# One core, DeltaNet then a normalised MLP: another order of the kernel's 3032 steps, with one filler less

## The chip, the cores and the metric

One core of one Trainium2 chip. The metric is the device time of the core in microseconds. The kernel before was timed three times: the median is 517.51 us, the lowest time 514.65 and the highest 519.48.

## The reference

All data are fp32. An attention block without softmax (the delta rule) is followed by a layer norm and an MLP with a residual.

```
q, k, v: (4 batches, 8 heads, 768 tokens, 48)   beta: (4, 8, 768)
k_n = k / (norm(k) + 1e-6); state = 0
for t in range(768):
    y[t]  = q[t] @ state
    state = state + beta[t] * outer(k_n[t], v[t] - k_n[t] @ state)
x   = y with heads joined               # (4, 768, 384)
xn  = (x - mean) / sqrt(var + 1e-6) * g_ln
out = x + relu(xn @ w_ch1) @ w_ch2      # 384 -> 1536 -> 384
```

## The kernel before, in words

The 768 tokens are cut into 12 chunks of 64. A chunk holds 64 tokens of all 4 batches, so 256 rows; its two halves (g = 0 and g = 1) are the 128 rows of two batches each. Inside a chunk the sequential rule becomes a triangular system: a Gram matrix of the keys, the inverse of a unit lower triangular matrix, products of that inverse with the values (u), and products of u with the queries' block (y). Only a state of 48 x 48 per head goes from chunk to chunk.

Chunk 0 has no state before it and nothing to overlap with, so it is done first and by itself. Its inverse is built in five doubling rounds on TensorE (products E1 to E5 and Z1 to Z5, lines 769 and 785), with masked copies and transposes on VectorE (lines 774 and 734) and copies out of PSUM on ScalarE (line 728), for two groups of eight heads in turn. Chunk 1 uses a Gram matrix that goes out to DRAM and comes back by rows (tile `gb`), and a row-by-row inverse on VectorE (lines 896 to 913). The later chunks use the same row-by-row inverse, in pairs, in five such stages that VectorE works through while TensorE does the MLP of earlier chunks. From chunk 3 on the MLP products are made from sums and differences of blocks, formed on VectorE and GpSimd (lines 1289, 1329, 1509, 1547), with fewer products on TensorE (lines 1306 and 1522).

The MLP weights are loaded and written anew as sums of two parts, by ScalarE (lines 591 and 599), VectorE (596) and GpSimd (609). The first MLP products of a chunk are 12 of 6 matmuls; in chunk 0 they are made for each half by itself, 24 in all (line 1405), each followed by a ReLU on ScalarE (line 1413).

**The order.** The kernel is first written down as a list of steps, numbered 0 to 3031. A step is one group of instructions on one engine (32 matmuls, one copy, one DMA) with the steps that must be done before it. Nothing of this list is executed in the order of its numbers: the string `ORDER`, some 100 lines of step numbers and ranges, says in which order the steps are emitted, and `Line.emit` goes through it word for word. It asserts that every step comes once and after all it depends on. `in_this_order` (line 23) then holds every engine to this order, and all DMAs of SP and ScalarE to one order among each other. So the engines run side by side, each through its own queue, and what the string decides is which step stands ahead of which in each queue.

Two words of the string are no steps. "f" and "F" are **fillers** (function `idle`, line 1595): a matmul of the identity matrix into a bank that the next TensorE step overwrites anyway, over 128 columns for "f" and 512 for "F". They compute nothing.

```
        n = 512 if size == "F" else 128
        nc.tensor.matmul(banks_of[key][:, 0:n], ident, ident[:, 0:1].to_broadcast([128, n]))
```

One more thing follows from the order: GpSimd's computing steps wait for the last VectorE step ahead of them in the string that is marked `port`, the normalising step of line 1150 among them (the dependency "shared port" in `Line.emit`).

The steps that the change and the prediction speak of:

| steps | engine, line | what they do |
|---|---|---|
| 201, 197 | TensorE 785 | last products of chunk 0's inverse (Z5), one for each group of heads |
| 181-183, 187-189; 198-200, 202-204 | ScalarE 728 | copies of Z4 and of Z5 out of PSUM |
| 191, 193 | VectorE 774 | last masked copies of the inverse |
| 236, 240, 242 | ScalarE 591, 599 | weight conversions over 768 columns |
| 259 | ScalarE 882 | square root on chunk 1's rows, waits for the loads of `gb` |
| 305 | SP 409 | one load of later keys (tile `kr`) |
| 329, 331 | TensorE 1068 | u of chunk 0, first and second half |
| 330, 332 | VectorE 1073 | scaling of u |
| 333, 334 | TensorE 1094 | y of chunk 0 (its output), first and second half |
| 335, 336 | ScalarE 1132 | y out of PSUM into x |
| 337-346 | VectorE, ScalarE | layer norm of both halves; 343 and 346 (line 1150) write the normalised halves |
| 309, 310, 321, 322 | TensorE 627 | key transposes of chunks 2 and 3 |
| 311, 312, 323, 324 | ScalarE 632 | the copies of these |
| 313, 325 | TensorE 818 | Gram products of chunks 2 (G2) and 3 (G3); 314, 315 and 326, 327 copy them out (ScalarE 839) |
| 353, 354 | TensorE 1104, ScalarE 1116 | state after chunk 0, and its copy |
| 426, 427 | TensorE 627 | query transposes of chunk 1 (428, 429 copy them, ScalarE 632) |
| 347, 351 | TensorE 1182 | transposes of the normalised first and second half |
| 348-350, 352 | ScalarE 1198, VectorE 1188 | the scaled transposes, copied out of PSUM |
| 567, 569, 571, ... 589 | TensorE 1405 | chunk 0's first MLP products, first half; 591 to 613 those of the second |
| 213, 217, 225, 229 | GpSimd 609 | last step of the conversion of four parts of the first weight |
| 366, 372, 378, ... | GpSimd 609 | the same for the second weight |

Of the kernel before, what the change touches and what calls it, by code (L numbers as in the profile page):

```python
# [174 lines left out]
682 781 1082 647 651 648-649 683-686 689 688 690 1084 1086 1069 837-838 833-834 843 793 1175 923 928 920 925 927 919 691 545-546  # L175
692-696 687 697 650 698-700 795 839 550 549 548 547 551 555 554 840 552-553 1091 1081 1083 845-846 848 847 1079 829-830 854 796
835 797 855-856 800 836 844 801 798 929 652 701 930 1176 931 643-644 1179 1181 628 1182 1172 1171 921 1183 918 629 1178 1180
1184-1185 556 802 702-704 1075 841 857-859 799 932 557 922 842 805 705 806 706-709 803-804 849-850 852 851 1085 463 864-868 860
871 933 807 810 559 561 558 869 560 934 811 808 710 809 812 562 872 861-862 1542 853 863 870 813 817 881 873-875 882 876 883-886
565-566 814 563 818 820 711-712 936 1087 877 713-716 564 816 815 819 935 937-938 879 1544 1554 887 1556 880 1553 888 1546 1543 878  # L180
1558 1560 1541 464 1555 1559 1557 1547 889-893 896 894 897 972 898-901 939 941 1186 717-722 895 723-725 902 940 726 1076 974
942-943 1077 975 907 1190 1088-1089 973 908-910 980-981 911-912 978 727-741 946 986 742 944-945 947 743-751 913 979 951 984-985
952 976 987 977 990-991 948-949 982 1005 992 983 988-989 1006-1010 994 1368-1370 1372 1367 1373 1078 1090 1371 1363 752 1095 1093
755-756 753 1545 1177 999-1000 996-997 1002 903 964-965 998 1012 970 1003 1013 904 967 995 1011 1187 953 955 754 915 1374 1094 757
950 954 758 1092 1650 905 956 1375 1188 1362 1653 906 1364 759 993 1022-1026 1030 1001 1004 1014 1096-1100 1102 760 762 1032
1015-1018 1033 761 763 766 1189 1034-1036 1019 1027 1037 1020 767 765 764 1103 1191 768 1192-1193 971 969 966 1219 1548 1021
1040-1045 769 1194 1652 914 960 1104 1028 1038 1196 1647 957-958 1655 959 1657 1360-1361 1029 1031 1039 968 1105 1047-1050 771-773
770 1106 1046 1058-1060 1107-1111 1195 774 1376 1198 963 962 1197 961 1199 1201-1202 1200 1549 1220 1234 1061-1062 1051 1227 1223
1238 1221 1366 776 1206 777 1203 778 1052 775 1228 1063 1207 1112 1377-1378 1208 1053 1064 1231-1232 1235 1659 1365 1656 1658 1654
1239 1236 1229-1230 1237 1055 1246 1224 1242 1247 1222 1225 1379 1210 1561 1204-1205 1380 1113 1381 1240 2030 1261 1233 1209 1660  # L190
1241 1114-1117 1243 1248 1244 1249 1245 1262 1275 1280 1270 1054 1226 1250 1118 1255 1258 1256 1259 1257 1382 1263-1264 1266-1267
1265 1260 1271-1272 1251 1119 1268 1281-1282 1273 1120-1121 1269 1283 1122-1124 1066 1211 1845 1212-1214 1284 1274 1308-1309 1057
1841 1215 1218 1065 1056 1844 1847 1849 1851 1646 2042 1252 1285 1253 1286 1310 1276 1383 1311 1277 1287-1288 1312 1298-1299 1254
1313 1278 1314 1292 1289-1291 1295-1296 1305 1300-1302 1333 1325-1326 1303-1304 1279 1334-1335 1315-1316 1336 1293 1306 1327 1294
1297 1337-1338 1307 1328 1317-1318 1329-1330 1322 2044 1323 1319-1320 1648 1850 1645 1839 1125-1129 1384 1339 1130-1131 1331 1324
1351-1356 1217 1216 2032 1332 1340-1343 1550 1344-1345 1415 2029 1419 1408-1410 2034 2033 1423 1551 1562 1411 1563 2031 1132-1135
1357 1385 1661 1424 2035 2046 2043 1136-1137 1321 1412-1413 1427 1138-1142 1346 1143-1165 1552 1564 1837-1838 1166 1567 1569 1566
1169 1168 1167 1170 1414 1416 1420 1417 1425 1418 1426 1432 1439 1421 1440 1433 1428-1430 1451 1442 1461 1443 1348 2036 1456 1422
1436-1437 1431 1438 1387 1444-1445 1447-1448 1101 1441 1434 1446 1435 1449 1452-1454 1457 1462-1463 1651 1565 1464 1450 1386 1455
1458 1479-1480 1466-1467 1481 1489 1482-1483 1490 1484 1491 1465 1662 1473 1347 2045 1470-1471 1674 1568 1388 1390-1391 1485 2047  # L200
1389 1468-1469 1474 1472 1476 1475 1459 1663-1664 2037 1395 1392 1667 1665 1460 1570 1666 1492-1494 1496-1499 1350 1349 1358 1848
1393 1396 1394 1397 1495 1571 1399 1398 1676 1668-1669 1671 1670 1672-1673 2041 1514 1500 1515 1477 1516 1486 1501 1487 1675 1677
1506-1509 1478 1488 1510-1511 1517 1503 1843 2048 1504 1518-1519 1649 1359 1846 1400 1402 1852 1401 1404 1403 1855 1572-1574 1577
1576 1512 1578 1502 1678 1681 1520 1683 1579-1580 1407 1405 1679 1406 1505 1513 1682 1704 1680 1686-1687 1691 1581-1585 1532-1533
1521-1523 1534 1524-1525 1705 1535-1536 1856 1853 1526 1586-1588 1684 1589 1685 1590-1591 1857-1860 1537 1706 1708 1692 1854 1709
1719 1715 1711 1723 1866 1861 1592 1527-1528 1707 1710 1538 1688 1863-1864 1862 1712-1713 1716-1717 1714 1720-1722 2049 1593 1747
1724 1529 1725-1726 1728 1840 2141 2135 2143 2145 1540 2328 1738 1757 1752 1739 1689-1690 1594 1694 1718 1727 1868 1732 1729 1733
1735-1736 1734 1740-1741 1743-1744 2142 2147 1530 2140 1842 2144 1531 2146 2137 1539 2133 1595 1693 1695-1696 1698-1699 1697 1700
# [1543 lines left out]
```

## Time and profile before

| | us |
|---|---|
| median of three runs (lowest, highest) | 517.51 (514.65, 519.48) |
| the execution that was profiled | 517.98 |
| its span in the trace | 516.2 |
| mean granted TensorE clock | 0.982 |
| TensorE busy | 484.4 (94% of the span) |
| VectorE busy | 360.4 (70%) |
| GpSimd busy | 280.4 (54%) |
| ScalarE busy | 206.5 (40%) |

The profiled execution took 0.47 us more than the median; some 1.8 us of it lie outside the span. The profile gives busy times and waits of each engine, and the trace behind it every instruction. A wait is named after what ended it; "issue" means that an engine stood still for nothing that the profile shows.

### The profile page before, as it was taken

The numbers are of one execution on the slowest core, as the hardware profiler recorded it, in microseconds if no ns is written. First come the engines' busy times: TensorE is split into PE (matmuls) and PEld (weight loads), VectorE is DVE, ScalarE is ACT, GpSimd is POOL, SyncE is SP. The second block draws the span as 40 slices with busy tenths as digits, with TensorE's granted clock in tenths as the row PEclk, the third lists the DMA queues.
The fourth block names the chain that finished last, engine by engine and source line by source line (L and its number), as shares of the span: only waits on it lengthen the run. The fifth ranks groups of instructions, "written<-read, shape, count | busy, mean of one in ns | idle before, by whom it ended". The sixth has DMA issues, their size and how long they took to land.

```text
span 516.2 us, 22793 instructions
## 1 busy us (share of the span) xinstructions
PE 484.4 (94%) x9970; PEld 448.6 (87%) x9970; DVE 360.4 (70%) x814; ACT 206.5 (40%) x462; POOL 280.4 (54%) x447
## 2 busy tenths in 40 slices
PE   4576898999999999999999999999999999999997
PEld 4454798678898898999989999999999999999996
DVE  6685548798899579979778998877688527253241
ACT  4685654632542234232443441444423344434130
POOL 7033455263477598777592354555444723654544
PEclk9898699999999999999999999999999999999999
DMA  9978477488626845354743554733440702212011
GB/s 136 258 161 211 143 126 175 107 190 153 117 46 117 181 109 91 75 109 114 148 106 64 119 109 97 150 80 64 103 79 24 160 19 57 62 36 60 2 39 30
DMA packets 181635, 54.56 MB, mean 106 GB/s; under 512 B 164888, under 2 KB 177312, under 8 KB 181536
## 3 DMA queue, kind: packets, MB, share of 16 engines
q1 hardware_dynamic: 168512, 40.10, 38.1%
q10 hardware_dynamic: 10816, 9.83, 6.7%
q0 software_dynamic: 2208, 3.17, 3.8%
q8 instruction: 78, 1.28, 1.0%
q14 instruction: 21, 0.17, 0.1%
HBM read 36.30 MB, written 16.78 MB: 103 GB/s over the span
## 4 chain that ended last, share of the span: by engine, by line
PE 80%; DVE 6%; DMA 5%; issue 3%; SPq 2%; ACT 2%; POOL 0%; ACTq 0%; DVEq 0%; POOLq 0%
PE f L1522 27%; PE f L1306 21%; PE f L1425 6%; PE two L818 4%; PE f L1405 3%; PE f L1447 3%; SPq L409 2%; PE by L1032 2%; PE by L1094 2%; PE two L1032 2%; PE two L1104 2%; PE two L1087 2%; DMA gb<-gd 2%; DMA gd<-gsb 1%; PE f L627 1%
## 5 line engine op out<-in xcount | busy, mean ns | idle before, releaser
L1509 POOL TENSOR_TENSOR h_all<-h_all 128x256 f32<-128x256 f32 x99 | 72.0, 740 | 21.5 <-DVE tmp L906 10.2
L1522 PE MATMUL f<-w_sb,h_all 128*128 128x192 f32 x396 | 80.0, 329 | 0.0
L1522 PE MATMUL f<-words,h_all 128*128 128x192 f32 x396 | 78.5, 330 | 0.0
L1329 DVE TENSOR_TENSOR h_all<-f,h_all 128x512 f32<-128x512 f32 x72 | 48.7, 685 | 27.5 <-PE f L1306 20.4
L1522 PEld LDWEIGHTS f<-w_sb,h_all 128*128 128x128 f32 x396 | 65.3, 190 | 1.4 <-ACT h_all L1434 0.2
L1522 PEld LDWEIGHTS f<-words,h_all 128*128 128x128 f32 x396 | 65.0, 190 | 0.9 <-issue 0.2
L1324 ACT COPY h_all<-f 128x512 f32<-128x512 f32 x45 | 26.1, 586 | 74.0 <-PE f L1306 57.4
L913 DVE TENSOR_TENSOR xb<-xb,tmp 128x31 f32<-128x31 f32 (+19 forms) x139 | 52.8, 380 | 3.5
L1547 POOL TENSOR_TENSOR words<-h_all 128x128 f32<-128x128 f32 x66 | 29.4, 468 | 46.8 <-ACT h_all L1333 23.2
L906 DVE TENSOR_TENSOR tmp<-xb,gb 128x31 f32<-128x31 f32 (+19 forms) x139 | 49.7, 357 | 3.9 <-POOL xb L893 0.3
L1333 ACT ACTIVATE h_all<-h_all 128x512 f32<-128x512 f32 x54 | 33.0, 628 | 25.2 <-DVE h_all L1329 24.9
L409 POOL DMA_DIRECT2D tb<-in_k_dram x64 | 41.7, 656 | 0.3 <-issue 0.2
L1306 PE MATMUL f<-x_new,w_sb 128*128 128x128 f32 x288 | 39.6, 276 | 0.0
L1306 PE MATMUL f<-xnt,w_sb 128*128 128x128 f32 x288 | 39.0, 277 | 0.6 <-DVE h_all L1329 0.6
L1306 PEld LDWEIGHTS f<-x_new,w_sb 128*128 128x128 f32 x288 | 36.7, 192 | 0.1
L1306 PEld LDWEIGHTS f<-xnt,w_sb 128*128 128x128 f32 x288 | 35.8, 192 | 0.9 <-POOL ident L1289 0.7
L1425 PE MATMUL f<-xnt,w_sb 128*128 128x256 f32 x144 | 33.8, 383 | 0.0
L1425 PEld LDWEIGHTS f<-xnt,w_sb 128*128 128x128 f32 x144 | 26.7, 190 | 3.9
L609 POOL TENSOR_TENSOR w_sb<-words 128x768 uint32<-128x768 uint32 (+1 forms) x11 | 14.7, 1352 | 22.3 <-issue 15.0
L1522 PE MATMUL f<-w_sb,words 128*128 128x192 f32 x132 | 26.2, 332 | 0.0
L1540 DVE TENSOR_TENSOR o<-f,x 128x192 f32<-128x192 f32 x33 | 11.3, 349 | 20.0 <-PE f L1522 17.8
L1132 ACT COPY x<-by 128x384 f32<-128x384 f32 x23 | 10.4, 479 | 36.4 <-PE by L1094 22.6
(237 smaller groups left out, 997.3 us busy)
## 6 DMA issues: line engine op xcount, KB each, us to landing
words<-in_moe_w_ch_dram ACTq DMA_DIRECT2D x20, 384.0 KB, 5.2
gd<-gsb SPq DMA_DIRECT2D x11, 512.0 KB, 3.2
v<-in_v_dram SPq DMA_DIRECT2D x24, 192.0 KB, 4.6
kr<-in_k_dram SPq DMA_DIRECT2D x46, 96.0 KB, 3.5
out_dram<-o SPq DMA_DIRECT2D x46, 96.0 KB, 2.6
xld<-xlt SPq DMA_DIRECT2D x9, 384.0 KB, 2.6
xnt<-xld SPq DMA_DIRECT2D x36, 96.0 KB, 3.0
tb<-in_q_dram SPq DMA_DIRECT2D x40, 64.0 KB, 3.0
```

The source lines that it names most:

```text
L409: add(eng, cost, lambda: QUEUE[eng].dma_start(out=out_, in_=in_), r, w, bulk=n * ns / 16e3, np=n, **kw)
L818: nc.tensor.matmul(pair[hp][half(e ^ (hp & n)), (g * NP + j) * C : (g * NP + j + 1) * C], kt[drows(hp), l], rt[drows(hp), i],)
L906: lambda j=j, n=n, w=w, t=t: nc.vector.tensor_tensor(out=t, in0=xv[:, 0:n, j : j + 1].to_broadcast([128, n, w]), in1=gv[:, j : j + 1, j + ...
L913: "DVE", dve(n * w), lambda t=t, rest=rest: nc.vector.tensor_tensor(out=rest, in0=rest, in1=t, op=ALU.subtract),
L1306: nc.tensor.matmul(wide(p[:, f : f + 128]), w[:, f : f + 128], r, start=start and i == 0, stop=True, skip_group_check=True)
L1324: add("ACT", act(512), lambda: nc.scalar.copy(o, p), pk, ok)
L1329: add("DVE", dve(512), lambda: nc.vector.tensor_tensor(out=o, in0=x, in1=y, op=op), [*xk_, *yk], ok)
L1333: add("ACT", act(512), lambda: nc.scalar.activation(o, o, ACTF.Relu, scale=scale), [], ok)
L1425: nc.tensor.matmul(p[:, 0:TOK], w1_sb[:, t, f * 128 : (f + 1) * 128], xnt[:, t], start=(t == 0), stop=(t == KC - 1))
L1509: add(eng, cost, lambda: e.tensor_tensor(out=out_, in0=x, in1=y, op=op), r, w, port=2 if eng == "Pool" else 1, pr=-2)
L1522: lambda f=f, t=start and f == order[0]: nc.tensor.matmul(p[:, 0:D2], lhs(f), rhs[:, f], start=t, stop=(f == order[-1]), skip_group_check=True
L1547: lambda f=f + i: e.tensor_tensor(out=s3[f], in0=one(0, 0)[0](f), in1=one(1, 0)[0](f), op=ALU.subtract),
```

## The change

Only the string `ORDER` is another. Both strings hold each of the 3032 steps once. The one before has two fillers, "f" ahead of step 94 and "F" (two matmuls over 512 columns in the trace) ahead of step 334; the one after has one, "f" ahead of step 114.

Of TensorE's 954 steps 747 stand at another place of its queue, by 2.9 places on average; of VectorE's 814 steps 716, by 4.2; of ScalarE's 489 steps with its DMAs 368, by 2.7; of GpSimd's 443 steps 376, by 4.0; of SP's 332 DMAs 294, by 6.7. The last 60 steps of TensorE's queue stand in nearly the same order as before.

Where the first chunk goes over into its MLP, TensorE's queue reads, before and after:

```
before: 201 197 310 329 331 333 F 334 309 313 321 322 353 325 426 347 427 351 567 571 569 575 430 593
after:  197 201 329 310 309 333 331 313 321 322 353 334 325 427 426 347 567 569 571 430 351 575 593 579
```

On ScalarE the copies 187 and 181 go ahead of the square root 259, and the conversions 240 and 242 behind all six copies of Z4; 336 goes behind 354; 349 goes ahead of 428. On SP load 305 goes behind the loads of `gb`. On VectorE the norm of the second half (339, 340) goes behind the normalising step of the first (343). On GpSimd 213, 217 and 225 stand behind 343 and ahead of 229. The start of the string, where the words above stand:

```diff
--- before
+++ after
 ORDER = """
-51 53-54 52 65 9 57-58 56 55 308 63 319 398 62 306 67 66 320 7 64 10 249 11-12 2 15 14 22 13 18 0 42 8 61 40 46 654 44 41 43 60 59
-656 47 72 71 1 75-77 82 3 101-102 27 83 16 24 73 84 99 68 103 74 36 104 100 93 37 f 94 38 105-106 85 17 28 86 69 87 21 70 6 88 78
-19 79 23 20 116-117 80 118 81 110-111 120 39 107 121 108 97 119 124-125 132 25 112 134 122 90 137 135 218 205 113 230 115 133
-140-141 143 123 34 109 251 258 253 92 136 207 114 126-128 152 138 142 89 208 154 30 26 129-131 157 139 146 148 147 158 91 96 156
-155 144-145 232 150-151 220 95 149 98 206 224 305 255 257 252 256 254 395 405 317 307 402 401 396 399 318 404 48 45 49 209 153
-160-161 159 168 219 162 170 169 163 176 653 657 165 210 172 166 171 222 173 167 164 5 29 177 4 174-175 223 31-32 184 186 185 178
-231 180 179 192 190 212 226 238 188 259 182 189 181 240 183 187 225 233 221 658 50 33 193 191 260-262 194-195 201 197 236 203 242
-204 200 199 198 202 211 241 237 310 329 239 263 35 196 243 250 264 331 227 330 333 332 F 334 234-235 214 312 335 361 356 355 336
-265-266 215 337 267-272 339 273 340 338 274-294 309 311 313 362 216 314 344 315 341 321-322 353 323-324 244 228 354 342 295 343
-325-327 345 393 316 296 403 397 328 406 213 217 248 229 655 659 346 426 347 427 348 350 428 349 429 351 567-568 571 569 572 575
-666 660 302 300 299 304 467 298 468-469 303 301 466 297 400 394 352 430 593 245 431 246 570 573 247 365 576 407 579 432 363 357
-359 465 668 358 360 364 580 594 583 599 584 574 367 661 410 587 577 588 368 578 591 581 592 582 366 408-409 600 411 470 585 379
-412 586 605 597 589 606 369 590 374 598 371 413 380 611 603 595 434 471-474 477 476 478-480 370 481 414 482 415 372 670 667 672
-671 665 669 392 461 1068 1070 416 433 604 596 601 418 373 419 612 602 420 417 609 607 385 421 608 610 386 381 383 377 613-614 422
-424 423 425 375 389 615-618 630-631 435-436 632 619 633 620 783 785-787 782 784 788 917 387 437 440 442 438 475 483-502 382
-503-506 376 507-515 673 439 378 384 634-635 662 441 443-444 447 445-446 663 516 388 517 450-452 448-449 518 621-622 674 789 1174
-779-780 664 1173 1080 390 462 1072 1067 1071 391 1073 677 1074 790 519 457 453 636-641 675-676 916 520-539 681 678 924 540 680 679
-926 542 541 544 543 459 456 458 455 460 454 623 791 794 821 624-625 642 822 645-646 792 825 827 626-627 826 831-832 823-824 828
...
+52 0-1 54-55 53 51 58 57 393 56 66 320 67 63 62 308 398 306 319 65 9 61 10 59 64 249 7 5 11-14 2 44 8 40 654 60 42 45 41 43 46 248
+656 71-72 68 38 75 82 76 3 101-102 36 83-84 74 77 39 37 73 100 99 6 21 85-86 69 28 16 24 22 70 78 15 17 23 79-80 27 87 81 88 116
+18 110-111 117 19 112 103-106 93 89 122 94 207 90 f 114 107-108 120 115 113 92 121 119 206 97 109 251 253 258 118 124 31 30 20 123
+125-127 32 130 132 128 134 133 136 135 137 129 220 131 218 232 230 138 33 139-141 143 142 146 152 25 34 219 147 153 26 148 158 154
+231 91 96 222 145 144 151 156 150 157 149 208 155 95 226 228 98 214 160 159 162 223 161 164 163 168 170 29 174 169 4 176 171 167
+166 165 172-173 205 210 254 252 395 255-257 402 307 305 401 318 405 317 48 233 653 49 658 175 50 221 47 177-178 181 179 184 186
+185 192 238 236 187 259 189 188 182-183 240 242 180 190 193 191 194-195 197 201 200 198-199 235 204 203 202 209 260 211 261 241
+262-263 237 35 250 265 329 234 310 196 330 309 311 264 243 362 333 312 239 331 335 224 356 361 355 266-273 332 274 337-338 275-285
+215 286-293 313-315 321 216 322 246 353 334 212 323-324 341 244 354 342 294-295 343 336 325-327 427 426 347 316 396 399 406 296
+403 328 217 213 225 227 339 348 350 349 428 340 344-345 567 407 568 429 229 659-660 666 245 346 408 247 655 657 404 300 303 301
+304 298 466 468 299 302 467 297 469 400 397 394 569 571 570 572 430 351-352 357 363 431 575 593 576 579 573 580 583 432 409 359
+584 587 574 594 358 364 360 410 577 588 599 591 367-368 578 581 411 365-366 592 582 585 600 605 597 470 412 586 589 598 413 369
+590 379 595 371 596 374 603 661 667-668 1068 434 465 471-474 477 476 478-479 370 480 414-415 372 670-672 392 665 669 391 601 416
+606 602 604 419 418 380 611 417 612 420 373 609 607 630 433 421 385 610 608 381 386 383 424 423 422 375 425 377 631-633 615-616
+634 617 635 435-436 618-620 783 785 787-788 916 481-509 376 382 378 437 440 389 441 387 442 438 673 510-514 384 1070 439 445 388
+446 515 443 450 516-517 451 518-520 444 782 789 636-637 613 662 638-639 614 663 447 674-675 786 784 780 390 790 521 452 448-449
+522-539 779 917 664 1176 676 924 680-681 540 679 678 925-926 542 541 543-544 621-623 457 624 453 625 640-641 1072 1080 1071 1082
+458 456 460 459 455 454 794 791 626 642 821-822 645 792 627 646-647 475 648-649 651 825 827 826 831 823 832 828 837 682 833 838
+843 834 683-686 689 781 677 688 845 1069 1084 848 1074 922 463 1079 1073 1067 1086 1081 1085 824 846-847 1083 545 793 546 839 547
+550 548-549 551 554-555 553 552 829 840 830 652 690 556 687 795 927 921 928 918 920 919 923 929-930 691-695 931 650 696-701
...
```

More of the change, by code (lines that the diff above doesn't have):

```diff
@@ L177 @@
[L177 to L184, printed above, removed]
@@ new lines @@
+1173 1185 1184 841 857 932 557 858-859 851 849-850 842 807 1075 1541-1542 853 464 861 864-865 559 703 808 933 810 860 871-872 809
+813 811 704-706 812 852 863 862 1544 878 560-561 558 562 934 817 881 873-874 882 866-869 883-884 875-876 885-886 819 816 566 563
+818 820 814 564-565 815 1087 1554 1546 936 707-712 887 713-714 877 870 715-716 935 937 1556 879-880 461-462 1543 1545 1547 1186
+889-894 896-901 972 1091 888 717-722 938 723-724 939-940 895 902 941 1076 973 943 942 1077 907 974-975 908-912 1190 1088 980-981
@@ new lines @@
+978 986 979 1089 984-985 987 725-728 946 729-736 947 737-751 913 976 990 977 982 944-945 948-949 991 1005-1007 983 988 992 1008
+989 994 1009 951 993 995 1368 1172 1361 1369-1370 1372 1078 1371 1367 1648 1360 1374 752 915 1090 755 754 756 753 1094 1558 1560
+1559 1557 1548 996 903 1177 997 999 904 1187 964 998 1002 970 1000 1003 1012-1013 967 1092 914 905 1093 1174 1095 906 969 952 757
+953 950 1188 954-955 758 1015 1032-1033 1010 1034 1016-1018 1001 1004 965 1220-1221 1014 1011 1022 1019 1023-1024 760-762 759 768
@@ new lines @@
+1189 763 1191 971 966 1219 1366 1020 1035 1021 1036-1037 1040-1041 1096 765 767 766 764 1038 1047 956 1649 1039 1553 1373 960 957
+1365 958-959 1192 1048 1025 1042 1026-1027 1043 769 1375 968 1193-1194 772 771 770 961 963 1549 1653-1655 1657-1659 1656 1364 1652
+1029 1097-1100 1102 962 1234 1223 1030 1028 1227 1103-1104 1195 1031 1196 1044-1045 1049-1052 1046 1224 1053 773 1197 774 777-778
+775 1198-1200 1055 1270 1238 1376-1377 1201-1203 776 1204 1058-1063 1228 1231 1206 1064 1235 1229 1236 1232 1239-1240 1237 1242
@@ new lines @@
+1644 1641 1643 1927 1919 1924-1926 1876 1824 1930-1931 1825 1949 1944 1939 1932 1928-1929 1933 1935-1936 1934 1937 1940-1941 1945
+1950-1951 1938 1878 1942 1879 1883 1922 1943 1977-1980 1967 1952 1946 1954-1955 1968-1970 1923 1971 1953 1884 1877 1885 1887
+1880-1882 1956 2151 1947 1957-1959 1961-1962 1964 1974 2139 1963 1826 2054 2337 1827 2055 2057 2149 2152 2150 1886 2156 1972 1981
+1973 2155 1948 2154 2058 2153 1888 1836 2339 1835 2334 2338 2135 1891 1889-1890 2522 1892 1960 1965 1975 1966 1976 1982 1994-1995
@@ new lines @@
+1983-1985 2002-2003 1986 1991 2157 2162 2159 2059 1987-1989 2004-2007 2164 2053 2060-2061 2343 2062 2064-2065 2008 2066 1996
+2160-2161 2158 2163 2165-2166 1893 2020 1997-1999 2021 2167 2169 1990 2067-2069 2340 2070-2071 2000 1992 2001 1993 2063 2072 2168
+1895 2170 2172-2173 2171 2192 2174 1894 2176-2177 2073 2178 2199 2203 2175 2179 2009-2012 2022-2025 2193 2013-2014 2196-2197 2074
+2015 2200 2194 2201 2075-2076 2195 2180-2181 2016-2017 2207 2235 2211-2212 2026 2183 2077 2341 2344 2204-2205 2198 2226-2227 2202
@@ new lines @@
+2342 2182 2206 2078-2079 2525 2527 2184 2529 2524 2530 2027 2187 2517 2531 2711 2330 2528 2185-2186 2188 2018-2019 2526 2028
+2208-2209 2216 2213-2214 2210 2080-2081 2215 2082-2085 2345 2347 2346 2220-2221 2223 2222 2348 2228 2224-2225 2229 2217 2231-2232
+2086-2088 2230 2233 2236-2237 2218 2238 2349 2354 2245 2331 2240 2246-2247 2234 2219 2239 2241 2273 2242 2263 2089-2091 2248
+2092-2094 2250-2251 2274 2356 2252 2352 2351 2249 2350 2253-2254 2257 2255-2256 2264-2267 2353 2260 2258 2095-2097 2275 2268
@@ new lines @@
+2600 2621 2617 2622 2618 2623 2630 2601 2631 2602 2515 2568 2571 2569-2570 2516 2572 2632 2740 2734 2736 2657 2626 2658 2647-2648
+2659 2649-2650 2634-2635 2633 2603 2651-2652 2739 2741 2636 2627 2653 2628 2637 2660-2662 2664-2668 2574-2575 2742 2638 2641
+2639-2640 2645 2504 2506-2507 2655 2644 2654 2674 2743 2573 2766 2773 2809 2642-2643 2663 2646 2656 2675-2677 2682 2767 2683-2684
+2678 2685-2687 2679 2671-2672 2669 2688 2768 2700-2701 2680 2670 2673 2689-2690 2770 2702 2691 2781 2769 2782 2703-2704 2692-2694
@@ L253 @@
+2976 2983-2984 2987-2988 2985 2951 2964 2961-2963 2967 2965-2966 2968 2977 2989 2978 2990-2992 2889 2888 2986 2997-3000 3005 2898
+2897 3006-3007 2969 2979 3001-3002 3008 2994 3003-3004 2996 3009 3012-3014 3010 3015-3017 2995 3011 2993 3018 3023-3029 3020 3019
+3021 3030 3022 3031
 """
```

115 lines of the change are left out of this document (45 added, 70 removed).

## The prediction

> **What bounds the kernel now.** I read the page first for the engine that sets the end, then a table of stretches for the place where that engine stands idle, then the timeline of that place, engine by engine.
>
> ```profile
> span 516.2 us, 22793 instructions
> PE 484.4 (94%) x9970; PEld 448.6 (87%) x9970; DVE 360.4 (70%) x814; ACT 206.5 (40%) x462; POOL 280.4 (54%) x447
> q8 instruction: 78, 1.28, 1.0%
> PE 80%; DVE 6%; DMA 5%; issue 3%; SPq 2%; ACT 2%; POOL 0%; ACTq 0%; DVEq 0%; POOLq 0%
> kr<-in_k_dram SPq DMA_DIRECT2D x46, 96.0 KB, 3.5
> ```
>
> TensorE is busy 94% of the span and makes 80% of the chain that ended last, so the end moves only if TensorE's idle time shrinks or grows: the change removes no work but one filler. The stretches (length, then busy time of PE, PEld, DVE, ACT, POOL, then granted clock, DMA share, GB/s) say where it idles.
>
> ```profile
> 0.00:42.40 42.40, 25.63 (x866) 21.24 (x866) 31.29 (x86) 28.78 (x68) 18.12 (x35) 0.96 0.91 182
> 42.40:64.20 21.80, 16.22 (x353) 13.28 (x354) 11.30 (x44) 12.02 (x27) 8.26 (x12) 0.69 0.63 180
> 50.98:61.22 10.24, 8.88 (x221) 7.82 (x216) 6.88 (x30) 6.30 (x12) 2.71 (x4) 0.50 0.50 159
> 64.20:512.40 448.20, 442.58 (x8754) 414.12 (x8752) 317.47 (x684) 165.68 (x369) 253.98 (x402) 1.00 0.45 95
> 182.00:208.00 26.00, 25.62 (x797) 23.52 (x797) 23.19 (x37) 10.37 (x28) 21.79 (x26) 1.00 0.47 94
> ```
>
> Up to 42.4 us (chunk 0's inverse) TensorE is idle for 16.8 us, from there to the first MLP product at 64.2 for 5.6 us and at a clock of 0.69, and in the 448 us after it for 448.20 - 442.58 = 5.6 us. From 64.2 on there is almost nothing to win and much to lose; what comes earlier ahead of 64.2 shows at the end almost whole. The timeline of TensorE around it:
>
> ```profile
> 40.03 1.04 PE L785 MATMUL f<-xt,pt 64*64 64x64 f32 x55 [0.69 <-ACT xt L728]
> 42.03 0.35 PE L785 MATMUL f<-xt,pt 64*64 64x64 f32 x9 [0.97 <-issue]
> 42.50 0.66 PE L627 MATMUL f<-ident,kr 128*128 128x128 f32 x4
> 43.78 0.83 PE L1068 MATMUL two<-v,xt 64*64 64x48 f32 x32 [0.62 <-ACT xt L728]
> 44.33 1.14 PE L1068 MATMUL by<-v,xt 64*64 64x48 f32 x32
> 45.27 1.10 PE L1094 MATMUL two<-u,pt 64*64 64x48 f32 x32
> 46.30 1.73 PE L1599 MATMUL by<-ident 128*128 128x512 f32 x2
> 47.97 0.44 PE L1094 MATMUL by<-u,pt 64*64 64x48 f32 x15
> 50.80 0.58 PE L1094 MATMUL by<-u,pt 64*64 64x48 f32 x17 [2.40 <-issue]
> 51.32 1.11 PE L627 MATMUL f<-ident,kr 128*128 128x128 f32 x4
> 53.10 1.98 PE L818 MATMUL f<-kt 48*64 48x64 f32 x64 [0.67 <-ACT kt L632]
> ```
>
> Two waits here are "issue": 0.97 us at 42.03 and 2.40 us at 50.80, the second in the middle of 334's 32 matmuls. Between their ends stand 9+4+32+32+32+2+15 = 126 matmuls, each with a weight load, so about 252 instructions. The page's instruction queue moved 1.28 MB in 78 packets, 16.4 KB each. I read both waits as instruction blocks that arrive late, and place them by count of instructions, not by step.
>
> **The change part by part.** *T1, end of the inverse.* The last products (201, 197) wait for ScalarE's copies of Z4 and for VectorE's last masked copy:
>
> ```profile
> 38.17 0.78 DVE L774 COPY_PREDICATED pt<-u,two 128x512 f32<-128x512 int32 x1
> ...
> 37.19 1.16 ACT L728 COPY xt<-f 64x256 f32<-64x256 f32 x3 [0.49 <-DVE qt L734]
> 38.24 0.95 ACT L591 ACTIVATE words<-words 128x768 f32<-128x768 f32 x1
> 39.22 0.76 ACT L728 COPY xt<-f 64x256 f32<-64x256 f32 x2
> ...
> 29.14 3.42 SPq L409 DMA_DIRECT2D gb<-gd  x5
> ```
>
> The copies end at 39.98, because a conversion of 0.95 (240) stands among them. Afterwards it stands behind all six, so they end at 39.98 - 0.95 = 39.03, level with the masked copy (38.95). The 55 matmuls took 1.04 us and the other 9 took 0.35: 39.03 + 1.39 + the block wait of 0.97 = 41.39 in place of 42.38, a gain of **1.0**. Bounds: 0, if the block comes no earlier than now, to 2.0, if its wait goes too. The square root 259 now has four copies queued behind it, and it waits for `gb`; five of these loads were issued up to 32.56 and 305 no longer stands ahead of them, so I take nothing for it. 305 itself brings keys that are transposed at 42.50 at the earliest; from its new place (after 32.6) the page's 3.5 us to landing leave 6 us of cover.
>
> *T2, the second block wait.* From the first wait's end the new queue has 9+32+4+4+32+32 = 113 matmuls ahead of G2 (313), so the block ends with 13 of G2's 64. The other 51 follow at 50.80: 51/64 x 1.98 = 1.58, G2 ends at 52.38. Before it ends at 53.10 + 1.98 = 55.08, since the rest of 334 (0.58), the transposes 309 (1.11) and the wait for their copy (0.67) came after the block. A gain of **2.7**; if all 64 come after it, 2.3. I let the block move along with T1; if it lands at 50.80 whatever TensorE does, T1 is lost in it.
>
> *The filler.* It takes 1.73 us at 46.30, but the 2.40 us of block wait behind it hides that: without it 334 would only have stopped earlier. I take **0**. If that cover went, leaving it out would gain 1.7; what it may do for the clock is a rival below.
>
> *T3, from G2's end to the first MLP product.* Before, 64.19 - 55.08 = 9.1 us.
>
> ```profile
> 61.78 0.49 PE L1182 MATMUL by<-ident,xln 128*128 128x128 f32 x3
> 62.11 0.60 PE L627 MATMUL two<-ident,tb 128*128 128x128 f32 x4
> 63.81 0.55 PE L1182 MATMUL by<-ident,xln 128*128 128x128 f32 x3 [1.10 <-ACT xnt L1198]
> 64.19 0.83 PE L1405 MATMUL f<-xnt,w_sb 128*128 128x128 f32 x6
> 65.45 2.27 PE L1405 MATMUL f<-xnt,w_sb 128*128 128x128 f32 x18 [0.43 <-ACT h_all L1413]
> ...
> 62.88 0.60 ACT L632 COPY qt<-two 128x512 f32<-128x512 f32 x1
> 63.35 0.41 ACT L1198 ACTIVATE xnt<-by,g_sb 128x128 f32<-128x128 f32 x1
> ...
> 58.51 1.72 POOL L609 TENSOR_TENSOR w_sb<-h_all 128x384 uint32<-128x384 uint32 x2 [13.48 <-DVE rstd L1147]
> ```
>
> 334 now lies in here whole: 32/17 x 0.58 = 1.09. 427 (0.60) goes ahead of the transposes 347. In return 349 no longer stands behind a query copy (0.60). Sum **+1.1**; bounds 0 (TensorE waits for ScalarE here anyway) to +1.7 (the query copy only changes places). The transposes still need 334 and its copy 336, which is now behind 354 on ScalarE; that is the same bank as before. The GpSimd conversions stand behind the first half's norm as before, now three (0.86 each); the first product needs two, 1.7 us behind the norm against some 5 us from norm to product, so nothing.
>
> *T4, the first MLP products.* 571 used to wait 0.43 for the ReLU on the bank of 567; now 569 stands between them: -0.4. The second half's transposes (351) go from the wait at 63.81 into the dense part: the first product can start 0.38 earlier, the dense part gets 0.55 more. Together **-0.2**.
>
> *T5, everything after.* All moves are inside queues, and TensorE has only 5.6 us of idle left, so **0**; bounds -3 (half of it goes) and, upwards, the VectorE rival.
>
> Sum: -1.0 - 2.7 + 1.1 - 0.2 = -2.8 against the profiled execution's own 517.98 us: 515.2. That execution lies 0.47 above the median of 517.51, so the forecast is **514.7**, own range 511 to 518.
>
> **The rivals.** *A. The block waits shrink.* The 0.97 and 2.40 us go, as the blocks land before TensorE asks for them: 514.7 - 0.97 - 2.40 = **511.3**. For it: of the 78 packets only two show as such a wait in this stretch. Against it: the same loads are in flight, and without the filler TensorE asks earlier. The Trainium skill ("Runtime: NRT & Kernel Launch", Instruction fetch mechanics) says that the sequencer fetches the next block of 256 instructions while it executes the current one and that crossing a block is mostly hidden. The count of 252 agrees; the 2.40 us at 50.80 do not.
>
> *B. The lead is eaten by the second weight.* What TensorE gains it may have to wait for GpSimd, whose conversions of the second weight come no earlier, being held in their queue:
>
> ```profile
> 100.86 2.89 POOL L609 TENSOR_TENSOR w_sb<-words 128x768 uint32<-128x768 uint32 x2 [9.85 <-issue]
> ```
>
> Then the second layer's products start when they start now: 514.7 + 2.8 = **517.5**. For it: 366 to 378 have nearly the same neighbours in GpSimd's queue. Against it: GpSimd stood idle 9.85 us ahead of that row.
>
> *C. The clock stays low for longer.* Of the 21.8 us ahead of 64.2, 10.24 ran at half clock:
>
> ```profile
> 59.41 1.94 PE L818 MATMUL f<-kt 48*64 48x64 f32 x64
> ...
> 67.66 1.16 PE L818 MATMUL two<-qt,kt 48*64 48x64 f32 x64
> ```
>
> The same 64 matmuls take 1.94 there and 1.16 at full clock. With the filler gone TensorE has 1.73 us less work in the idle stretch ahead. If one more half-rate stretch of that length falls into dense MLP products, it costs 10.24 x (1 - 1.16/1.94) = 4.1: **518.8**, slower than before. Against it: the products begin dense, and the clock had risen by 61.22 before they began. The Trainium skill ("TensorE: Matmul & The Clock Gate", What's actually happening) has the clock at half after an idle window of about 3.4 us and back at full after one busy window; it speaks for keeping fillers, but by it one more window would cost 3.4 x 0.40 = 1.4 us, an estimate, which gives 516.1. The trace's stretch lasted 10.24 us, three times that, with 1.4 us of idle in it.
>
> *D. VectorE falls behind in the row-by-row inverses.* This ends on the other side. In 182 to 208 us VectorE is busy 23.19 of 26.00 us beside a TensorE at 25.62, so it has 2.8 us of slack in a stage, and its queue takes everything in order: a PSUM sum (line 1329) behind four more steps of the inverse holds a bank, and TensorE behind it. The diff moves VectorE's steps by 4.2 places on average; at 360.4/814 = 0.44 us each that is 1.9 us. If each of the five such stages pays that once, 9.3 us: 514.7 + 9.3 = **524.0**. It decides where a step with a waiting bank goes back by more than 2.8 us, six places. For it: some steps move by up to 77 places. Against it: moves go both ways, and 5.6 us of idle in 448 show that the order before leaves room.
>
> **How the numbers follow.** Chances: forecast 0.42, A 0.19, B 0.12, C 0.10, D 0.17. The range goes from 508 (A with T5's bound of 3) to 523, which leaves out the upper half of D and little else. A measurement here can tell about 1%, 5.2 us, from no change, so faster begins at 512.3 and slower at 522.7. Faster: most of A (0.16) and the lower part of the forecast's own range with T1 in full and T5 helping (0.18), 0.34. Slower: most of D (0.14) and a tail of C (0.04), 0.18. The same: 0.48.
>
> **What would show it.** T1: the last Z5 matmul ends near 41.4. T2: the second block wait lies inside G2 (line 818), not in line 1094, and G2 ends 2.7 us plus T1 earlier, near 51.4. T3 and T4: the first line 1405 row starts near 61.2, and no wait for a ReLU stands behind it. T5: idle of TensorE after that about 5.6 us still. A shows as no "issue" wait over 0.5 us, B as a TensorE wait for line 609, C as a clock below 1.00 behind the first MLP product, D as TensorE waiting for lines 1329 or 913 behind 90 us. The prediction is wrong if TensorE's idle behind the first MLP product changes by more than 3 us, or if that product comes no earlier.

## The result, and the profile after

| order | median us (runs) | before, same runs | ratio to before, 95% interval |
|---|---|---|---|
| after | 513.09 (22) | 515.83 (22) | 0.9944 [0.9917, 0.9971] |
| after, second measurement (e10) | 510.34 (6) | 516.88 (29) | 0.9908 [0.9876, 0.9939] |

The new order is faster by 0.6% and, in a second measurement, 0.9%. The forecast was 514.7 against 517.51, a ratio of 0.9946. The ratios leave disturbed runs out and the medians don't, so for some experiments below (e1 and e4 most) the two differ by some tenths of a per cent.

The profiled execution of after took 512.30 us, so it lies 0.79 below its median, and the one of before 2.15 above that of the larger sample. Of the 5.6 us between the two spans only about half is the change by the medians of the same runs (2.7); by the second measurement it would be more than all of it (6.5). Nothing here shows why the two measurements lie 3.8 us apart. Its page:

```profile
span 510.6 us, 22793 instructions
PE 482.3 (94%) x9968; PEld 448.7 (88%) x9968; DVE 358.2 (70%) x814; ACT 206.3 (40%) x462; POOL 282.2 (55%) x447
PE 85%; DVE 7%; issue 2%; DMA 2%; SPq 2%; ACT 1%; POOL 0%; DVEq 0%; ACTq 0%; POOLq 0%
```

TensorE has two matmuls less (the filler) and makes a larger part of the chain; DMA and "issue" make a smaller one. The stretches up to the end of chunk 0's inverse, from there to the first MLP product, and 450 us from there on (columns as in the prediction's table):

```profile
0.00:45.55 45.55, 28.01 (x884) 24.40 (x886) 29.85 (x87) 28.96 (x69) 17.99 (x36) 0.85 0.85 174
45.55:58.96 13.41, 10.60 (x344) 9.27 (x336) 10.30 (x40) 10.51 (x22) 4.07 (x5) 0.87 0.75 224
58.96:509.00 450.04, 443.71 (x8755) 414.99 (x8755) 318.05 (x687) 166.83 (x372) 260.18 (x408) 1.00 0.47 97
```

The inverse ends at 45.55 instead of 42.38, which is 3.2 us later. The stretch behind it takes 13.41 us instead of 64.19 - 42.38 = 21.81, which is 8.4 shorter. From the first MLP product to the end of the span it is 510.59 - 58.96 = 451.6 against 516.24 - 64.19 = 452.1, which is 0.4 shorter. So in this pair almost nothing of the gain comes from where most of the steps were moved; it is a gain in one stretch, and a loss ahead of it. The experiments show that the pair is not typical of the part behind the first product. TensorE in that stretch:

```profile
42.39 1.12 PE L785 MATMUL f<-xt,pt 64*64 64x64 f32 x53
45.11 0.39 PE L785 MATMUL f<-xt,pt 64*64 64x64 f32 x10 [1.59 <-issue]
...
46.39 1.44 PE L627 MATMUL f<-ident,kr 128*128 128x128 f32 x8 [0.38 <-ACT xt L728]
47.76 1.11 PE L1094 MATMUL two<-u,pt 64*64 64x48 f32 x32
48.65 1.07 PE L1068 MATMUL by<-v,xt 64*64 64x48 f32 x32
49.50 1.74 PE L818 MATMUL f<-kt 48*64 48x64 f32 x64
51.91 1.14 PE L627 MATMUL f<-ident,tb 128*128 128x128 f32 x8 [0.67 <-ACT gsb L839]
52.99 1.15 PE L1104 MATMUL two<-u,kr 64*64 64x48 f32 x64
53.95 0.28 PE L1094 MATMUL by<-u,pt 64*64 64x48 f32 x3
55.44 0.61 PE L1094 MATMUL by<-u,pt 64*64 64x48 f32 x27 [1.21 <-issue]
...
58.96 2.50 PE L1405 MATMUL f<-xnt,w_sb 128*128 128x128 f32 x18 [0.55 <-ACT xnt L1198]
```

G2 (line 818 at 49.50) now stands ahead of 334 (line 1094 at 53.95) and runs without a break. The block wait in front of it is gone; one of 1.21 us has come into 334, one block further on. Behind 58.96 the 18 products follow each other with no wait for a ReLU. ScalarE in the same stretch, where the issues of weight loads (ACTq) share its queue with the copies:

```profile
47.87 0.58 ACT L632 COPY kt<-f 128x512 f32<-128x512 f32 x1 [1.13 <-PE f L627]
47.95 0.60 ACTq L409 DMA_DIRECT2D words<-in_moe_w_ch_dram  x1
48.59 0.58 ACT L632 COPY kt<-f 128x512 f32<-128x512 f32 x1
48.99 0.55 ACTq L409 DMA_DIRECT2D words<-in_moe_w_ch_dram  x1
...
49.59 1.30 ACTq L409 DMA_DIRECT2D words<-in_moe_w_ch_dram  x2
51.27 1.07 ACT L839 COPY gsb<-f 128x512 f32<-128x512 f32 x2 [1.27 <-PE f L818]
```

All four issues are over (50.89) when G2 ends at 51.24, and the copies of its banks follow at once. In e7 and e9 below they do not.

### The profile page after: what moved, and what is told of

It reads as the page before. It is cut to its first block, busy times and chain, and to the rows that moved or that the text cites. A ratio compares the mean times of both kernels' runs of the same rounds, so it can differ in the third digit from the quotient of the medians.

```text
span 510.6 us, 22793 instructions
## 1 busy us (share of the span) xinstructions
PE 482.3 (94%) x9968; PEld 448.7 (88%) x9968; DVE 358.2 (70%) x814; ACT 206.3 (40%) x462; POOL 282.2 (55%) x447
## 4 chain that ended last, share of the span: by engine, by line
PE 85%; DVE 7%; issue 2%; DMA 2%; SPq 2%; ACT 1%; POOL 0%; DVEq 0%; ACTq 0%; POOLq 0%
PE f L1522 31%; PE f L1306 21%; PE f L1425 6%; PE two L818 4%; PE f L1447 3%; PE by L1032 2%; PE two L1032 2%; PE by L1094 2%; PE two L1087 2%; PE two L1104 2%; PE f L785 2%; PE f L1405 2%; SPq L409 2%; DVE tmp L906 1%; DVE xb L913 1%
## 5 line engine op out<-in xcount | busy, mean ns | idle before, releaser
L1522 PE MATMUL f<-w_sb,h_all 128*128 128x192 f32 x396 | 81.1, 331 | 0.0
L1522 PE MATMUL f<-words,h_all 128*128 128x192 f32 x396 | 76.7, 329 | 0.0
L906 DVE TENSOR_TENSOR tmp<-xb,gb 128x31 f32<-128x31 f32 (+19 forms) x139 | 52.7, 379 | 4.0 <-POOL xb L893 0.4
L609 POOL TENSOR_TENSOR w_sb<-words 128x768 uint32<-128x768 uint32 (+1 forms) x11 | 14.8, 1348 | 19.4 <-ACT words L599 10.1
L1289 POOL TENSOR_TENSOR x_new<-xnt 128x128 f32<-128x128 f32 x27 | 12.8, 479 | 22.2 <-DVE rstd L1147 6.6
```

Of the source, the lines that this page charges most:

```text
L906: lambda j=j, n=n, w=w, t=t: nc.vector.tensor_tensor(out=t, in0=xv[:, 0:n, j : j + 1].to_broadcast([128, n, w]), in1=gv[:, j : j + 1, j + ...
L1522: lambda f=f, t=start and f == order[0]: nc.tensor.matmul(p[:, 0:D2], lhs(f), rhs[:, f], start=t, stop=(f == order[-1]), skip_group_check=True
```

## The experiments

All of them change only the string `ORDER`. Each was timed beside runs of before; the medians are of 12 runs each, 6 for e10. The traces were also cut into the parts used above; the table at the end gives them.

**e1: the filler alone.**

```diff
-331 227 330 333 332 F 334
+331 227 330 333 332 334
```

> Order of before, only the filler F left out. My theory (the filler lies under the 2.40 us instruction-block wait in 334): the time of before within 1 us, and the block wait at the 1986th TensorE instruction grows to about 4 us. Rival (the missing filler is the gain): 2 to 3 us below before.

Measured: 518.10 against 518.30 of before, ratio 1.0049 [1.0011, 1.0088]. No gain, so the missing filler is not the cause. The way it is hidden is not as I had put it, though:

```profile
44.63 0.49 PE L785 MATMUL f<-xt,pt 64*64 64x64 f32 x9 [2.22 <-issue]
51.90 0.68 PE L1094 MATMUL by<-u,pt 64*64 64x48 f32 x15 [1.99 <-issue]
```

The wait in 334 did not grow to 4 us. It fell to 1.99, and the one a block earlier was longer. From wait to wait it is 7.27 us here and was 8.77 before: in this pair of profiles the block came sooner when TensorE asked sooner.

**e2 and e11: the filler back in the new order.**

```diff
-353 334 212
+353 F 334 212
```

> Order of after, with the filler F put back ahead of 334. My theory: there the wait for a block is 1.21 us and PE is otherwise dense, so at most 0.5 us of the filler's 1.0 to 1.7 us shows: after plus 0 to 0.5. Rival (the missing filler is the gain): back at before, 2.7 us above after.

> Order of after with F ahead of 334, now beside after on the same chip. Theory F (the filler shortens the time at half clock): 1.5 to 3.5 us below after, with fewer microseconds at half clock. Rival (the filler does nothing; e2 and after differed since they were measured at different times): within 1 us of after.

Measured: e2 512.28 against 518.30, ratio 0.9927 [0.9888, 0.9965]; e11 511.24 against 516.88, ratio 0.9923 [0.9894, 0.9952], with the unchanged after in the same runs (e10) at 510.34:

> The order of after unchanged, beside the other kernels of this call, as their measure: 2 to 4 below before.

It came out 6.5 below before, more than expected. After e2 the filler seemed to gain 3 us; measured side by side it does not. That theory fell: in the new order the filler does nothing that can be measured. In the order of before the medians say the same (e1, 0.2 us apart), and the ratio of e1 has the kernel without it 0.5% slower; neither shows a gain from leaving it out.

**e3, e4: where along the order the gain is made.** The string is cut at the first MLP product (567).

```diff
 e3: order of after up to 567, then what is left in the order of before
 e4: order of before up to 567, then what is left in the order of after
```

> Order of after up to the first MLP product (567), what is left in the order of before. My theory (all of the gain is made ahead of the first MLP product): the time of after within 1 us, so 2 to 4 below before; in the trace the first MLP product near 59 as in after. Rival (the later order makes the gain, or gives part of it back): within 1 us of before; or, if the later order gives back, 2 us below after.

> Order of before up to the first MLP product (567), what is left in the order of after. My theory: the time of before within 1 us. Rival (the later order makes the gain): 2 to 3 below before.

Measured: e3 514.48 and e4 517.86 against 518.30; ratios 0.9955 [0.9921, 0.9989] and 1.0049 [1.0004, 1.0094]. So the order up to the first MLP product gains without the later one. The reverse does not follow from e4, since where its two halves meet it has a wait that neither before nor after has:

```profile
67.55 0.22 ACT L1016 ACTIVATE knrm<-ksum 128x16 f32<-128x16 f32 x1 [2.92 <-DMA ksum<-gd]
67.98 0.94 PE L1405 MATMUL f<-xnt,w_sb 128*128 128x128 f32 x6 [2.70 <-ACT h_all L1413]
```

The square root of line 1016 stands ahead of ReLUs, as in after, but the last load that it needs is issued as late as in before (62.56; in after 54.41). ScalarE waits for it, and TensorE 2.70 us for the ReLU behind it. A better measure of the later order is e2 against e3, timed in the same runs: they differ in the later order and in the filler, and e2 is 2.2 us lower (1.0 to 3.7, a 95% interval from resampling the runs). So the later order is worth about 2 us where the start is that of after. In the profile of e3 the first product starts at 63.98 and not near 59: that execution had the longest inverse of all (47.59).

**e5, e6, e12: the start and the inverse.** The string is cut at the end of the inverse.

```diff
 e5:  order of before up to 197, then that of after
 e6:  order of after up to 201, then that of before
 e12: e5 with F ahead of 334
```

> Order of before up to the end of chunk 0's inverse (197), then the order of after. In the profiles the inverse ended at 42.38 us before and 45.55 after. Theory I (the order of after makes the start and the inverse 3 us slower): 3 us below after, near 510, the inverse ends near 42.4. Theory II (the 3 us are the clock and the loads of that one execution, not the order): the time of after.

> Order of after up to the end of chunk 0's inverse (201), then the order of before. Theory I: 3 us above before, near 519, the inverse ends near 45.5. Theory II: the time of before.

> Order of before up to the end of the inverse (197), then that of after, with F ahead of 334. Theory I (the new order of the loads and of the head groups at the start costs 2 us): 2 us below the kernel of the same order with the start of after (F ahead of 334 in both), the inverse ends near 44 instead of 45.7. Rival: the same as that kernel.

Measured: e5 511.89 against 516.77, ratio 0.9918 [0.9882, 0.9954]; e6 517.21 against 516.77, 1.0017 [0.9979, 1.0056]; e12 511.45 beside e11's 511.24 in the same runs. e3 and e6 have the same order up to the inverse's end and behind the first product, and differ between them: e3 is 3.8 us below its before and e6 0.4 above, so that stretch is worth about 4 us by the medians, and 3 by the ratios. (e5 and e4 differ in it as well, by 4.4 us, but of this up to 2.7 can be the wait shown for e4.) On the start the traces are clear and the times are not. In the seven profiles whose start is that of after, the first product of the inverse (E1) begins at 17.14 to 17.19 us, in the seven with the start of before at 14.48 to 15.69. The rows of before and after:

```profile
14.63 0.69 PE L769 MATMUL by<-qt,gsb 64*64 64x64 f32 x32 [1.39 <-DVE ndb L661]
```

```profile
7.07 1.94 PE L627 MATMUL by<-ident,kr 128*128 128x128 f32 x8 [7.07 <-DMA kr<-in_k_dram]
17.14 1.13 PE L769 MATMUL two<-qt,gsb 64*64 64x64 f32 x32 [3.06 <-DVE qt L757]
```

In after the first transposes wait for chunk 0's keys, of which SP now issues one quarter (51) third instead of first; and VectorE works on both head groups' masks and transposes (110 to 118) in turn, so that the first group is ready later. At the end of the inverse 1.6 us of it are left (45.58 against 43.98 on average). But e12, with the earlier start, is not faster than e11. Theory I holds for the stretch and is not shown for the whole; an effect of 1 us is below what these runs can tell.

**e7: G2 first, alone.**

```diff
-333 332 F 334 ... 312 335 ... 309 311 313
+333 332 309 312 335 311 313 334
```

> Order of before with only this changed: 309, 312, 335, 311 and G2 (313) stand ahead of 334, and the filler F is left out. My theory (G2 behind the rest of 334 and the block wait was the late step; T2 of the prediction): G2 ends 2.7 us earlier, the time 1.5 to 2.7 below before. Rival (334 has to be done before the first MLP product anyway, so G2 ahead of it only swaps the two): within 1 us of before.

Measured: 517.31 against 516.77, ratio 0.9989 [0.9949, 1.0029]. The rival is right about the time, but not for its reason. G2 does end early, 6.2 us behind the inverse as in after (5.7), and then TensorE stands still:

```profile
47.43 1.41 PE L818 MATMUL f<-kt 48*64 48x64 f32 x63 [0.68 <-ACT kt L632]
51.66 1.97 PE L627 MATMUL f<-ident,tb 128*128 128x128 f32 x8 [2.31 <-ACT gsb L839]
```

It waits for the copies of G2's banks, and ScalarE's queue shows what stands ahead of them:

```profile
47.89 1.95 ACTq L409 DMA_DIRECT2D words<-in_moe_w_ch_dram  x3
49.94 0.48 ACT L1132 COPY x<-by 128x384 f32<-128x384 f32 x1 [1.56 <-DVE xb L913]
49.97 0.57 ACTq L409 DMA_DIRECT2D words<-in_moe_w_ch_dram  x1
50.59 0.55 ACT L599 ACTIVATE h_all<-h_all 128x384 uint32<-128x384 uint32 x1 [0.17 <-issue]
51.04 0.57 ACT L839 COPY gsb<-f 128x512 f32<-128x512 f32 x1
```

Four issues of weight loads, the second half's copy (336) and a conversion, up to 51.04, though G2 was done at 48.89.

**e9: the whole second half set back as well.**

```diff
+ 334 behind 353; 336 behind 354; 339 340 behind 343; 348 350 349 344 345 346
  (on top of e7; the loads 361 356 355 362 stay ahead of 314)
```

> Order of before with the second half's output, its copy and its norm set back on all queues: 334 behind 353 on TensorE, 336 behind 354 on ScalarE, 339 and 340 behind 343 on VectorE, 344 to 346 behind the first half's scaled copies; G2 as in e7, the filler F left out. Theory M (G2 alone gave nothing because ScalarE's copy 336, which needs 334, still stood ahead of the copies of G2's banks; with both set back the gain of the stretch comes): the stretch from the end of the inverse to the first MLP product is 14 to 15.5 us, against 19.5 us on average with the order of before, and the time is 3 to 5 below before. Rival (the gain needs the rest of the new order there, conversions and key copies too): within 1.5 us of before.

Measured: 516.45 against 516.88, ratio 0.9992 [0.9955, 1.0030]. Theory M fell: passing the first half ahead on all three engines gives nothing by itself. The profiled execution took 522.12 us, 5.7 above the median, but what it shows on ScalarE is a matter of order, and the same as in e7:

```profile
51.17 3.21 ACTq L409 DMA_DIRECT2D words<-in_moe_w_ch_dram  x4
54.43 0.55 ACT L599 ACTIVATE h_all<-h_all 128x384 uint32<-128x384 uint32 x1 [2.78 <-issue]
54.88 1.05 ACT L839 COPY gsb<-f 128x512 f32<-128x512 f32 x2
```

336 is out of the way, and the four issues and the conversion behind them hold the copies up until 54.88, 2.2 us after G2's end at 52.70. The edit lacks what after has: the load issues spread into ScalarE's idle time ahead of G2's end.

**e8: the four loads later still**, in the new order.

```diff
-311 ... 362 ... 356 361 355 ... 334 ...
+311 ... 334 ... 336 362 356 361 355 325
```

> Order of after, with four loads of the second weight (355, 356, 361, 362; 384 KB each) moved behind 334. Theory (instruction blocks arrive late because these loads fill the DMA queues): the block wait inside 334, 1.21 us in after, goes and with it 1 us of the time. Rival (blocks arrive late whatever else is loaded): that wait stays over 0.8 us and the time is that of after.

Measured: 515.22 against 516.77, ratio 0.9982 [0.9951, 1.0013], so most of the gain of after is gone. The wait inside 334 went as expected, and the time did not. The issues now stand ahead of the copies that the first MLP product needs:

```profile
49.29 1.03 PE L818 MATMUL f<-kt 48*64 48x64 f32 x52 [0.61 <-issue]
...
59.63 2.50 PE L1405 MATMUL f<-xnt,w_sb 128*128 128x128 f32 x18 [2.13 <-ACT xnt L1198]
```

```profile
56.03 2.07 ACTq L409 DMA_DIRECT2D words<-in_moe_w_ch_dram  x3
58.15 1.07 ACT L839 COPY gsb<-f 128x512 f32<-128x512 f32 x2 [2.04 <-POOL w_sb L609]
59.11 0.90 ACT L1198 ACTIVATE xnt<-by,g_sb 128x128 f32<-128x128 f32 x3
```

The copies at 58.15 had waited 2.04 us, the length of the three issues, though their products were done at 56.15; the row's named releaser had long been done. The first product waits 2.13 where in after it waited 0.55. All the same, the whole stretch from the inverse to the first product is 14.6 us, no longer than with the order of after (table below). The loss lies behind it: from there to the last second-layer product of chunk 0 (step 641) this kernel takes 53.0 us against 48.5 to 51.1 in the other seven with the same later order.

```profile
64.13 1.75 ACT L591 ACTIVATE words<-words 128x768 f32<-128x768 f32 x2 [1.68 <-DMA v<-in_v_dram]
...
66.08 2.27 PE L1405 MATMUL f<-xnt,w_sb 128*128 128x128 f32 x18 [0.79 <-ACT h_all L1413]
...
74.03 0.94 PE L1405 MATMUL f<-xnt,w_sb 128*128 128x128 f32 x6 [1.72 <-ACT h_all L1413]
```

By the trace the load issued at 57.47 landed at 64.04, and a conversion of the second weight waits for it on ScalarE (the row names another DMA). A ReLU stands behind this conversion, and TensorE waits 0.79 us for it. The second ReLU stands behind two more load issues, which start at 72.43 instead of 68.68. In after TensorE has neither wait.

**The parts in the profiles** (us; the average, and in brackets the range and the number of executions):

| part | order of before | order of after |
|---|---|---|
| first product of the inverse starts | 15.16 (14.48 to 15.69, 7) | 17.16 (17.14 to 17.19, 7) |
| end of the inverse | 43.98 (42.38 to 45.12, 7) | 45.58 (44.29 to 47.59, 7) |
| from there to G2's end | 11.24 (9.78 to 12.70, 4) | 5.94 (4.85 to 7.75, 7) |
| from there to the first MLP product | 8.26 (7.06 to 9.11, 4) | 8.83 (7.44 to 11.35, 7) |
| both together | 19.50 (16.85 to 21.81, 4) | 14.77 (13.41 to 16.38, 7) |
| of it at half clock | 10.1 (0.1 to 16.3, 4) | 4.8 (0 to 10.2, 7) |
| from the first MLP product to TensorE's last matmul | 449.7 (448.2 to 451.0, 4) | 445.6 (444.9 to 447.7, 6) |
| TensorE idle in it | 5.4 (5.1 to 5.6, 4) | 2.3 (1.6 to 4.0, 6) |

Each row goes by the order that a kernel has in that part. e7, e8 and e9, which mix the orders between the inverse and the first product, are left out below the first two rows, and e4 with its wait of 2.70 us in the last two.

Between the inverse and the first MLP product the ranges do not meet: 4.7 us less. Part of this is the clock. A fit of these eleven stretches by order and by time at half clock gives 3.5 us for the order and 0.23 us for each microsecond at half clock. e7 and e9, which move some of the steps, take 17.4 and 19.5, and e8 takes 14.6.

Behind the first product the ranges do not meet either: about 4 us less, 3 of it idle time of TensorE. The kernels with the order of before have 2.8 us more at half clock there, which by the 0.34 us worked out at the end is about 1 us, an estimate. Of the kernels left out, e4 takes 448.5, e7 446.0, e8 449.8 and e9 452.4, so e7 gets near the short ones with the later order of before. The largest single piece is a wait in line 980, here in before and then in e10:

```profile
86.25 0.54 PE L980 MATMUL f<-xnj,gsb 32*32 32x32 f32 x38 [1.81 <-issue]
```

```profile
80.15 0.87 PE L980 MATMUL f<-xnj,gsb 32*32 32x32 f32 x64
```

Of the six kernels with the later order of before five have it, with 1.25 to 2.05 us, and of the eight with that of after only one, after itself, has it over 0.5 us (1.49). Why the block comes in time in the others is not shown.

## Why the prediction was right or wrong

**The sum was right, and three of its terms were not.** The forecast was 2.8 us less and the two measurements gave 2.7 and 6.5. It came from 1.0 and 1.8 in two places and nothing behind them. The profiled pair has a loss of 3.2 and a gain of 8.4 there and a gain of 0.4 behind; the averages of the profiles have a loss of 1.6, a gain of 4.7 and a gain of about 4. That the first measurement met the sum is luck: errors of opposite sign cancelled. So is G2's end at 51.24, near the 51.4 that was forecast: the inverse ended 4.2 us later than forecast and G2 came 4.3 us sooner behind it.

**T1 failed, in sign.** I priced the copies ahead of the last products, and these do come without a conversion between them. The step that failed is that I gave no price to the start of the string, where the order of the key loads and of VectorE's first steps had changed as well: E1 begins later in every kernel with that start, by 2.0 us on average. From E1 to the end of the inverse it is 28.4 us against 28.8, so of the 1.0 that T1 priced 0.4 may be there, well within the scatter. Every instruction ahead of the place that I looked at belonged in the sum.

**T2 was right in kind and too small.** G2's end comes 5.3 us earlier behind the inverse on average, in place of 2.7 (7.0 in the profiled pair). I had the block wait cut G2 after 13 of its 64 matmuls. In e8 it does, after 12. In after it did not: the waits stand one block earlier, at 45.11, and one block later, in 334. G2 in after also ran partly at full clock, 1.74 us against 1.98.

T2 also left out ScalarE's queue: e7 does T2 alone and gains nothing in time, and in its trace G2's copies stand behind load issues there. The diff moves these issues too, and I followed none of them. That they are the whole reason is argued from the traces and not shown.

**The filler at 0** was right within what these runs can tell (e1, e11 against e10). Its cover was not the one I named, as the block wait shrank with the filler gone.

**T3**, +1.1, measured +0.6 on average (-1.4 in the profiled pair), with 334 whole inside the stretch as worked out. **T4**: the ReLU wait of 0.43 is gone.

**T5 failed in size.** It was put at 0, as all moves are inside queues, with a lower bound of -3. The profiled pair has -0.4, but e2 against e3 gives -2.2, and the idle time behind the first product goes from 5.4 to 2.3 on average, so a figure near that bound would have been right. The prediction named a change of more than 3 us in this idle time as a sign of being wrong: in the profiled pair it goes from 5.6 to 4.0, in e10, the same kernel in another execution, to 1.6.

**The rivals.** A did not come: in after five such waits of over 0.8 us stand before 60 us, where before had three. B and D: behind the first product TensorE in after waits nowhere for lines 609 or 913, and for line 1329 once, for 0.3 us. C: in the profile of after the clock is 1.00 from there on. Nearest to B comes e8, where the second weight's loads, issued later, cost TensorE 2.5 us behind the first product, but by way of ScalarE and not of GpSimd.

**What stays open.** Which set of the steps between the inverse and the first product is enough. e7 and e9 are not, e3 is. The traces of e7 and e9 point to the four load issues; e8, whose loss lies behind the stretch, does not settle it, and a kernel with e9 and only these four moved was not run. Open as well is which of the later steps bring the 2 us behind the first product, and how much the new start costs in time.

## What to carry to other kernels

A load that is issued from a computing engine's queue takes time of that queue (here 0.55 and 0.60 us for one, 3.21 for four): count it ahead of every copy that TensorE waits for, and place it where that engine is idle, but not so late that what needs the load waits (e8). Moving a product forward on TensorE gained nothing here while the copies that empty its bank came no sooner on the other engine (e7, e9). When a whole order is replaced, cut it at two or three places and swap the pieces; four kernels told more of where the gain was made than the reading of one stage, whose total was right by errors that cancelled. But look in the trace of each spliced kernel for a wait where its pieces meet, before its time is taken for that of a piece (e4).

## What the runs showed of the hardware

**Instruction blocks.** In the fourteen traces TensorE has 46 waits called "issue" of over 0.5 us in the first 66 us. 45 of them stand at the same few counts of TensorE's instructions (matmuls, weight loads and the waits for semaphores between them): 449, 705, 961, 1217, 1473, 1729, 1985, 2241 (a multiple of 256, less 63). Which of these wait, and for how long (up to 2.4 us), differs from execution to execution. Of the last three counts it was 1729 and 2241 in the profile of after, 1985 in e8, and 2241 alone with 2.17 us in e10, the same order as after. Such a wait can be placed by counting, but not predicted for one execution. Of what the Trainium skill says ("Runtime: NRT & Kernel Launch", Instruction fetch mechanics), the block of 256 instructions agrees with these counts. That crossing it is mostly hidden holds here for 67 of the 112 crossings at these counts; at the other 45 TensorE stood still for 0.5 to 2.4 us.

**The clock.** In these traces the granted clock falls to half for stretches of 3.41 us or a multiple (the last one is cut off by the end), and where they fall differs too. Before 62 us both profiled executions had 17.1 us of them: before at 16.8, 44.2 and 51.0 to 61.2, after at 16.3 to 23.1, 26.5 to 33.3 and 47.0. Of the 22 runs of after the time at half clock, worked out from span and mean clock, is 8 to 38 us, and their times from 508.92 to 521.01 follow it with 0.34 us for each microsecond (correlation 0.86). So the spread of 2.4% between runs of one kernel is larger than the change, and a single pair of profiles, here 5.6 us apart in span, cannot tell it.
